# Landing allowances for loads in a kernel's own scheduler: attention and two expert MLPs in fp32 on one Trainium2 core

## The chip, the cores and the metric

The kernel runs on one core of a Trainium2 chip. The metric is the device time of one execution in microseconds (us), as the median of several runs. The engines are named as in the profile: PE is TensorE (matmuls), PEld its weight loads, DVE is VectorE, ACT is ScalarE, POOL is GpSimd, and SP is SyncE, which here only issues transfers (its queue is SPq).

## What is computed

Three steps follow each other; the output of one is the input of the next. The sizes are B=4, H=8, S=576, D=64 for attention, and 2304 tokens, model width 512 and inner width 2048 for both MLPs. All arithmetic is in fp32.

```python
def attention(q, k, v, M_prev, z_prev, beta):
    scores = where(causal, -1e9, q @ k.T / sqrt(D))
    a = exp(scores - scores.max(-1)); a /= a.sum(-1) + 1e-9
    local = a @ v
    q_p = where(q > 0, q, exp(q) - 1) + 1
    mem_out = (q_p @ M_prev) / (q_p @ z_prev + 1e-6)
    g = sigmoid(beta)
    return g * mem_out + (1 - g) * local
def moe(x, w_in, w_out, s, b):
    r = maximum(x @ w_in, 0)
    return (s * r * r + b) @ w_out
def moe2(x, w_in, w_out, a, b):
    h = x @ w_in
    P = a[0] + a[1] * h + a[2] * h**2 + a[3] * h**3
    Q = 1 + abs(b[0]) * abs(h) + abs(b[1]) * h**2
    return (P / (Q + 1e-6)) @ w_out
```

## The kernel before, in words

**Arithmetic.** A fp32 product is made of three matmuls: each operand is split into a high part (a cast, lines 368 and 370) and a low part (the operand minus its high part, line 378, `pair_op`), and high times high, high times low and low times high are summed in PSUM. The weights of both MLPs come as 64-bit raw values. A raw block is one load of 512 KB, 128 x 1024 words (`dAi_..r`, `dAo..r`, `dB_..r`, `d2i_..r`, `d2o..r`). `decode` (from line 405) turns it into 128 x 512 fp32 values with one ACT instruction (line 418, into `..m`), four DVE instructions (lines 419, 421, 423, 425, into `..f`), a cast to the high part and a subtraction for the low part.

**Stages.** From 0 to about 407 us the 32 attention units run (4 batches, low or high queries, 4 pairs of heads): scores `s` (line 657), mask and maximum on DVE (`s,st`, line 664), exponentials `p` on ACT (line 675), transposes `pt`, copies `th`, the sum `av`, and the gated result `xp` on DVE (line 877), which multiplies with `cb`, a row of reciprocals that goes to DRAM (`crow`) and comes back broadcast over partitions. Between them PE runs a filler, block A: the first half of the inner width of MLP 1 for early blocks of 256 tokens (`ha`, line 922; on DVE `ha` at line 939 and `gla` at line 940; `acc`, line 987). Its weights are decoded in the first 110 us (16 raw blocks `dAi`, `dAo`); the other half of these weights is decoded in 16 raw blocks `dB`, one about every 16 us from 124.8 us on, and stored to DRAM. From about 407 us on the rest of block A runs, then block B (the second half of the inner width, 450 to 657 us; `hb`, line 922; `hb` and `glb` on DVE at lines 939 and 940), beside which the raw blocks of MLP 2 (`d2o`, `d2i`) are decoded, then block C (MLP 2, to the end).

**What sets the order.** Nothing in the program issues instructions in the order in which it is written. `Plan.op` (line 109) registers an operation with the engines that may run it (`ways`, each with a cost in us), the buffers it reads and writes, and a place in time (`at`). `Plan.run` then goes through all operations with a clock for every engine. For each engine `choose` takes, among the operations whose inputs have been given out, the one that can start soonest by the reckoned clock (ties by `at`); an operation with several ways is left to another engine if that one would end it sooner. What is chosen is issued at once, so the reckoned times set both the order of each engine's instructions and, for work that ACT, DVE or POOL could do, the engine. The chip then runs each engine's list in order and waits for real data.

A load on SP is reckoned so: SP is taken for 0.48 us; the data's share of the queue is `0.1 + size / 350e3` us; and its readers are ready at `o.end`:

```python
                clock[e] = start + 0.48
                dma = max(dma, start + 1.2) + cost
                o.end = dma + 1.2
```

For a raw block of 512 KB on an idle queue that is 4.0 us after the issue, for a broadcast load of `cb` of 96 KB 2.8 us. There are two buffers for raw blocks, and four PSUM banks (3 to 6) for the upward products `ha`, `hb`, `hc`; a bank of `hb` is given to a later group when DVE's `glb` has read it.

Of the kernel before, what the change touches and what calls it, by code (L numbers as in the profile page):

```python
# [39 lines left out]
}  # L40
PCOPY = False
RAW = 0
ALONE = 8
R0, R1, RN = 0.0, 0.0, 0
ENDS, LEAD, LEADS = 1, 0.7, 384
# [34 lines left out]
class Plan:  # L80
# [25 lines left out]
            t.obj = self.pools[t.place[0]].tile(t.shape, t.dt, tag=t.place[1], name=t.name, bufs=1)  # L106
        return t.obj

    def op(self, ways, fn, r=(), w=(), lag=0.0, port=False):


        o = Op(ways, fn, (self.at, len(self.ops)))
        o.ready = {e: self.since for e in ways}
        o.lag, o.port = lag, port
        keys = [(k, "r") for k in r] + [(k, "w") for k in w]
        keys = [(k if isinstance(k, tuple) else (k, None), x) for k, x in keys]
        deps, seen = set(), set()
        for (name, part), x in keys:
            t = self.bufs[name]
            assert not t.gone, name  # L120
            found = False
            for q, ops in t.did["w" if x == "r" else "r"].items():
                if part is None or q is None or q == part:
                    deps.update(ops)
                    found = True
            assert found or x == "w" or t.const, (name, part)
            if name in seen:
                continue
            seen.add(name)
            if t.before is not None:  # L130
                deps.update(t.before.users)
                t.before.gone = True
            if t.place is not None:
                if t.place[0] == "ps" and not t.users:
                    o.opens.append(t)
                elif t.place[0] == "ps":
                    deps.add(t.users[0])
                if t.place[0] in self.inner:
                    assert self.swap is None
                if t.place[0] in self.outer:  # L140
                    deps.add(self.swap)
        for (name, part), x in keys:
            t = self.bufs[name]
            if o not in t.users[-1:]:
                t.users.append(o)
                o.touch.append(t)
            t.did[x].setdefault(part, []).append(o)
        deps.discard(o)
        o.left = len(deps)
        for d in deps:  # L150
            d.next.append(o)
        self.ops.append(o)
        return o
# [10 lines left out]
    def run(self, engines, nbanks):  # L164
# [40 lines left out]
        for _ in self.ops:  # L205
            cand = [(c[1], c[2].at, e, c[2], c[3]) for e, c in ((e, choose(e)) for e in engines) if c is not None]
            start, _, e, o, b = min(cand, key=lambda c: c[:2])
            for x in o.ways:
                wait[x].remove(o)
            cost = o.ways[e]  # L210
            if e == "PE":
                busy = [x for x in busy if x[1] > start - 4.0]
                if sum(y - max(x, start - 4.0) for x, y in busy) < 2.6:
                    cost *= 2
                busy.append((start, start + cost))
            elif e != "SP":
                cost *= INFL
            if e == "SP":
                clock[e] = start + 0.48
                dma = max(dma, start + 1.2) + cost  # L220
                o.end = dma + 1.2
            else:
                clock[e] = start + cost
                o.end = clock[e] + o.lag
                if e == "POOL" or e == "DVE" and o.port:
                    port = clock[e]
            for t, i in zip(o.opens, b):
                bank_of[i] = t
                t.obj = self.pools["ps"].tile(t.shape, t.dt, tag=f"bank{i}", name=t.name)
            o.start, o.eng = start, e  # L230
            if o is self.swap:
                wait_for[0] = WAIT
            o.fn(engines[e])
            for t in o.touch:
                t.left -= 1
                t.free = max(t.free, o.end)
                if not t.left and t.place is not None and t.place[0] == "ps":
                    i = bank_of.index(t)
                    bank_of[i], bank_free[i] = None, t.free + BGAP
            for n in o.next:  # L240
                for x in n.ways:
                    n.ready[x] = max(n.ready[x], o.end + GAPS[e][x] + (SLACK if x == "PE" != e else 0.0))
                n.left -= 1
                if not n.left:
                    enlist(n)
# [3 lines left out]
def tile_kernel(ctx, tc, qk, vm, z, beta, w1i, w1o, s1, b1, w2i, w2o, a2, b2, out):  # L249
# [104 lines left out]
            t["POOL"] = 0.15 + c * 0.0021 * pool  # L354
        return t

    def load(dst, src, size, r=(), w=(), act=False):

        if act:
            op({"ACT": 0.55}, lambda e: e.dma_start(dst(), src()), r, w, lag=1.7 + size / 360e3)  # L360
        else:
            op({"SP": 0.1 + size / 350e3}, lambda e: e.dma_start(dst(), src()), r, w)  # L362

    def copy(dst, src, c, r, w, act=0.0, dve=1.0, pool=None):

# [41 lines left out]
    def decode(src, nm, hi, lo, key, total=False):  # L407

        ring(f"{nm}r", "raw", [P, 512, 2], I32)
        ring(f"{nm}m", "dm", [P, 512], F32)  # L410
        ring(f"{nm}f", "df", [P, 512], I32)
        R, M, F = f"{nm}r", f"{nm}m", f"{nm}f"
        load(lambda: g(R).rearrange("p f w -> p (f w)"), lambda: src.bitcast(I32), 512 * 1024, (), (R,))

        def top():
            return g(R)[:, :, 1]

        op(ways(512, 0.0), lambda e: e.activation(g(M), f32(top()), AF.Square), (R,), (M,))
        op(ways(512, None, 0.5), lambda e: e.tensor_scalar(
            g(F), top(), 3, 0x3FFFFFF8, ALU.logical_shift_left, ALU.bitwise_and), (R,), (F,), port=True)  # L420
        op(ways(512, None, 1.0), lambda e: e.scalar_tensor_tensor(
            g(F), g(R)[:, :, 0], 29, g(F), ALU.logical_shift_right, ALU.bitwise_or), (R, F), (F,), port=True)
        op(ways(512, None, 1.0), lambda e: e.scalar_tensor_tensor(
            g(F), top(), -0x40000000, g(F), ALU.bitwise_and, ALU.bitwise_or), (R, F), (F,), port=True)
        op(ways(512, None, 1.0), lambda e: e.scalar_tensor_tensor(
            f32(g(F)), g(M), TINY, f32(g(F)), ALU.is_ge, ALU.mult), (M, F), (F,), port=True)
        kh, kl = key
        copy(hi, lambda: f32(g(F)), 512, (F,), (kh,), dve=0.5, pool=0.41)
        pair_op(lo, lambda: f32(g(F)), lambda: f32(hi()), ALU.subtract, 512, (F, kh), (kl,))
        if total:  # L430
            pair_op(lambda: wsum, lambda: wsum, lambda: f32(g(F)), ALU.add, 512, (F, "wsum"), ("wsum",))
# [285 lines left out]
    def phi_b(p):  # L717
# [67 lines left out]
            load(lambda: crow[:, P:P + 64].unsqueeze(0), lambda: g(C1)[2:3].rearrange("o (j q) -> o j q", j=2), 1e4, (C1,), ((CR, 1),))  # L785
        for j in range(2):
            load(lambda j=j: g(CB)[64 * j:64 * j + 64], lambda j=j: crow[j:j + 1, 0:r.nq].to_broadcast([64, r.nq]),
                 64 * 4 * r.nq, (CR,), ((CB, j),))

    def transposes(n):  # L790

# [566 lines left out]
```

## Time and profile before

| | us |
|---|---|
| median of 3 runs | 1059.18 (1057.67 to 1060.86) |
| the profiled execution, its own time | 1057.09 |
| its span in the trace | 1055.1 |
| PE busy | 1016.8 (96% of the span) |
| DVE busy | 840.5 (80%) |
| ACT busy | 691.9 (66%) |
| POOL busy | 416.9 (40%) |
| share of PE on the chain of work that ended last | 69% |
| shares of DVE, DMA and ACT on that chain | 16%, 8%, 3% |

The span is the time from the first to the last instruction of one execution. PE is busy in nearly all of it. The chain of work that ended last is followed back from the last instruction, at each step to what released it; a DMA on it is a transfer for whose landing an engine waited while nothing else held up the end. A wait in a row of the profile is put down to the operation that ended it.

### The profile page before, as it was taken

How to read it: one execution, taken by the hardware profiler on the slowest of the kernel's cores; microseconds unless marked ns; L12 is line 12 of the kernel's file. 1: busy time of each engine (PE TensorE's matmuls, PEld its weight loads, DVE VectorE, ACT ScalarE, POOL GpSimd, SP SyncE). 2: the span in 40 equal slices, each digit the busy share in tenths (PEclk: the TensorE clock that was granted, in tenths of full speed). 3: DMA queues.
4: the chain of work that ended last, by engine and by line, in shares of the span. 5: the costliest groups of instructions: out<-in, count | busy, mean ns of one | idle time of the engine just before them, and what ended most of it. 6: DMA issues, size and time to landing. Idle time of an engine off the chain costs nothing.

```text
span 1055.1 us, 17519 instructions
## 1 busy us (share of the span) xinstructions
PE 1016.8 (96%) x5980; PEld 868.6 (82%) x5980; DVE 840.5 (80%) x1495; ACT 691.9 (66%) x1462; POOL 416.9 (40%) x473
## 2 busy tenths in 40 slices
PE   6879899989999999999999999999999999999998
PEld 4458688878977889987778999888888888898997
DVE  6989877887878875479999543888888888887896
ACT  6977665675557664355554444877866877777896
POOL 2412311122003131012021002877767876876785
PEclk8998999999999999999999999999999999999999
DMA  7766555556646656987765332900200200010000
GB/s 208 220 192 190 162 184 187 171 187 183 208 143 186 202 170 212 341 257 218 239 219 170 103 101 71 318 1 5 73 1 0 70 1 1 23 41 1 30 1 30
DMA packets 88632, 140.41 MB, mean 133 GB/s; under 512 B 12408, under 2 KB 50400, under 8 KB 88544
## 3 DMA queue, kind: packets, MB, share of 16 engines
q1 hardware_dynamic: 83856, 130.52, 39.3%
q0 software_dynamic: 4224, 8.39, 2.6%
q8 instruction: 47, 0.77, 0.3%
q10 hardware_dynamic: 464, 0.40, 0.2%
q14 instruction: 41, 0.34, 0.1%
HBM read 103.56 MB, written 35.71 MB: 132 GB/s over the span
## 4 chain that ended last, share of the span: by engine, by line
PE 69%; DVE 16%; DMA 8%; issue 3%; ACT 3%; SPq 1%; POOL 1%; DVEq 0%; ACTq 0%; POOLq 0%
PE hc L922 19%; PE ac L1113 19%; PE acc L987 7%; PE ha L922 7%; PE ab L1026 5%; PE hb L922 4%; PE av L866 2%; PE pt L525 2%; PE s L657 2%; DMA dAi_1r<-in_w1i 1%; SPq L362 1%; DVE s L664 1%; PE av L874 1%; PE su L691 1%; ACT p L675 1%
## 5 line engine op out<-in xcount | busy, mean ns | idle before, releaser
L1092 DVE RECIPROCAL qe<-qe 128x512 f32<-128x512 f32 (+2 forms) x82 | 242.6, 2959 | 49.5 <-POOL qe L378 49.2
L922 PE MATMUL hc<-xc_h,w2il 128*128 128x512 f32 (+1 forms) x320 | 117.8, 368 | 0.0
L922 PE MATMUL hc<-xc_h,w2ih 128*128 128x512 f32 (+1 forms) x320 | 117.8, 368 | 0.0
L922 PE MATMUL hc<-xc_l,w2ih 128*128 128x512 f32 (+1 forms) x320 | 117.7, 368 | 0.0
L378 POOL TENSOR_TENSOR qe<-qe,qb 128x512 f32<-128x512 f32 (+2 forms) x82 | 94.9, 1157 | 55.3 <-ACT qb L1077 54.5
L1113 PE MATMUL ac<-w2oh,ghc 128*128 128x512 f32 x288 | 112.6, 391 | 0.0
L1113 PE MATMUL ac<-w2ol,ghc 128*128 128x512 f32 x288 | 112.5, 391 | 0.0
L1113 PE MATMUL ac<-w2oh,glc 128*128 128x512 f32 x288 | 112.3, 390 | 0.0
L378 POOL TENSOR_TENSOR glc<-po,ghc 128x512 fp32r<-128x512 f32 (+2 forms) x82 | 94.9, 1157 | 22.9 <-ACT ghc L368 22.8
L378 POOL TENSOR_TENSOR pm<-pm,s 128x512 f32<-128x512 f32 (+2 forms) x82 | 95.2, 1161 | 17.5 <-ACT pm L1077 16.5
L987 PE MATMUL acc<-gha,w1olA 128*128 128x256 f32 x288 | 85.3, 296 | 0.0
L1083 ACT ACTIVATE s<-hc 128x512 f32<-128x512 f32 (+2 forms) x82 | 44.7, 545 | 61.1 <-PE hc L922 58.4
L987 PE MATMUL acc<-gla,w1ohA 128*128 128x256 f32 x288 | 82.6, 287 | 0.6 <-DVE gla L940 0.6
L987 PE MATMUL acc<-gha,w1ohA 128*128 128x256 f32 x288 | 82.5, 287 | 0.0
L675 ACT ACTIVATE p<-s,st 128x128 f32<-128x128 f32 (+3 forms) x128 | 66.6, 529 | 18.2 <-DVE st L664 18.0
L1077 ACT ACTIVATE pm<-hc,prm 128x512 f32<-128x512 f32 (+2 forms) x82 | 59.6, 727 | 22.6 <-DVE hc L1094 21.9
L525 PE MATMUL pt<-ident,p 128*128 128x128 f32 x320 | 59.4, 282 | 12.4 <-ACT th L368 6.2
L922 PEld LDWEIGHTS hc<-xc_h,w2il 128*128 128x128 f32 x320 | 60.1, 188 | 9.0 <-DVE po L1096 0.4
L922 PEld LDWEIGHTS hc<-xc_l,w2ih 128*128 128x128 f32 x320 | 60.1, 188 | 8.6
L922 PEld LDWEIGHTS hc<-xc_h,w2ih 128*128 128x128 f32 x320 | 60.0, 188 | 7.5
L1077 ACT ACTIVATE qb<-s,cq,b1abs 128x512 f32<-128x512 f32 (+2 forms) x82 | 62.7, 765 | 2.1 <-POOL qe L378 2.1
L664 DVE CUSTOM_DVE_ANT_0 s<-s,mask 128x128 f32<-128x128 f32 (+3 forms) x128 | 60.2, 510 | 4.7 <-PE s L657 3.7
(498 smaller groups left out, 2962.8 us busy)
## 6 DMA issues: line engine op xcount, KB each, us to landing
vm<-in_vm SPq DMA_DIRECT2D x16, 384.0 KB, 4.0
k<-in_qk SPq DMA_DIRECT2D x32, 144.0 KB, 3.8
x2p<-ev SPq DMA_DIRECT2D x18, 256.0 KB, 4.4
out_y<-ob SPq DMA_DIRECT2D x18, 256.0 KB, 2.0
qm<-in_vm SPq DMA_DIRECT2D x16, 256.0 KB, 3.1
w1d<-sh SPq DMA_DIRECT2D x16, 256.0 KB, 2.3
w1d<-sl SPq DMA_DIRECT2D x16, 256.0 KB, 2.3
w2d<-sh SPq DMA_DIRECT2D x16, 256.0 KB, 2.9
```

The lines of the kernel that those rows point to most:

```text
L378: op(ways(c, None, dve, pool), lambda e: e.tensor_tensor(dst(), x(), y(), alu), r, w, port=True)
L525: nc.tensor.transpose(dst[:, o:o + P], src, ident)
L657: nc.tensor.matmul(g(b)[:, o2:o2 + kb - ka], g(Q)[m, q], g(K)[m, ka:kb], start=True, stop=True)
L664: e.tensor_tensor_reduce(sp, sp, mask[:, m0:m0 + kb - ka], -scale, 3.0e38 if x == 0 else st[:, t:t + 1], ALU.add, ALU.min, st[:, t + x:t + ...
L675: e.activation(g(f"p{n}_{i}")[:, o:o + kb - ka], g(b)[:, o2:o2 + kb - ka], AF.Exp, scale=-1.0, bias=g(f"st{n}")[:, z_:z_ + 1], accum_out=g ...
L922: nc.tensor.matmul(hs(), m, y, start=c == 0 and k == 0, stop=c == KC - 1 and k == 2)
L987: nc.tensor.matmul(a, outp(y, f)[:, cs], g(z_)[:, us], start=f == 0 and k == 0 and c % 2 == 0, stop=f == HF - 1 and k == 2, skip_group_che ...
L1026: nc.tensor.matmul(g(ACC)[:, 0:w], outp(y, f)[:, cs], g(z_), start=f == 0 and k == 0, stop=f == HF - 1 and k == 2)
L1077: return lambda e: e.activation(g(dst)[:, ks], g(src)[:, ks], AF.Identity, scale=m, bias=b)
L1083: op(ways(c, -0.04), lambda e, ks=ks: e.activation(g(S2)[:, ks], g(HS)[:, ks], AF.Square), (HS,), part(S2))
L1092: op({"DVE": 0.07 + c * 0.00625}, lambda e, ks=ks: e.reciprocal(g(QE)[:, ks], g(QE)[:, ks]), part(QE), part(QE))
L1113: nc.tensor.matmul(g(ACC), g(x_)[:, ks], g(f"w2o{y}{i}")[:, o], start=f == 0 and q == 0, stop=f == NF - 1 and q == 2)
```

## The change

Three constants are added: an operation on SP is reckoned to be ready 0.6 us later (`LANDS`, the default of `load`, so for stores and most loads), a raw weight block 1.6 us later (`LANDS_RAW`), and a load of `cb` 0.8 us later (`LANDS_CB`). Loads that ACT issues keep their reckoning. SP's own clock and the queue's `dma` are unchanged. For a raw block on an idle queue the reckoned landing goes from 4.0 to 5.6 us after the issue.

```diff
+LANDS, LANDS_RAW, LANDS_CB = 0.6, 1.6, 0.8
...
-    def op(self, ways, fn, r=(), w=(), lag=0.0, port=False):
+    def op(self, ways, fn, r=(), w=(), lag=0.0, port=False, late=0.0):
...
-        o.lag, o.port = lag, port
+        o.lag, o.port, o.late = lag, port, late
...
                 dma = max(dma, start + 1.2) + cost
-                o.end = dma + 1.2
+                o.end = dma + 1.2 + o.late
...
-    def load(dst, src, size, r=(), w=(), act=False):
+    def load(dst, src, size, r=(), w=(), act=False, late=LANDS):
...
         else:
-            op({"SP": 0.1 + size / 350e3}, lambda e: e.dma_start(dst(), src()), r, w)
+            op({"SP": 0.1 + size / 350e3}, lambda e: e.dma_start(dst(), src()), r, w, late=late)
...
-        load(lambda: g(R).rearrange("p f w -> p (f w)"), lambda: src.bitcast(I32), 512 * 1024, (), (R,))
+        load(lambda: g(R).rearrange("p f w -> p (f w)"), lambda: src.bitcast(I32), 512 * 1024, (), (R,), late=LANDS_RAW)
...
-                 64 * 4 * r.nq, (CR,), ((CB, j),))
+                 64 * 4 * r.nq, (CR,), ((CB, j),), late=LANDS_CB)
```

No arithmetic is added or removed, and PE keeps its 5355 rows of code. What changes is the order on every engine, and the engine of 184 operations. The new line numbers are higher by one. Up to the tenth `xp` DVE has 342 rows before and 346 now, and among them 10 subtractions into `w1ilA` and `w1olA` (line 378) before and 15 now; the five came from POOL.

**The first raw block, on ACT.** `dAi_0m` is the first instruction that reads raw block `dAi_0r`; `p` are exponentials, `ph` the exponential of q, `rb` a copy of reciprocals, `th` the copies of transposed `p` for which PE waits. Before:

```order
L675 ACTIVATE p_1_248,rs_200<-s_1_0_209,st_197 128x384
L418 ACTIVATE dAi_0m<-dAi_0r 128x512
L675 ACTIVATE p_0_266,rs_267<-s_0_0_223,st_244 128x128
L587 ACTIVATE ph_273<-qm_202 128x384
L368 COPY rb_284<-rec_95 128x2x3x64
L368 COPY th_0_290<-pt_0_275 128x384
L368 COPY th_1_294<-pt_1_280 128x384
```

Now:

```order
L676 ACTIVATE p_1_246,rs_202<-s_1_0_211,st_199 128x384
L676 ACTIVATE p_0_257,rs_258<-s_0_0_225,st_248 128x128
L588 ACTIVATE ph_272<-qm_195 128x384
L419 ACTIVATE dAi_0m<-dAi_0r 128x512
L369 COPY th_0_291<-pt_0_274 128x384
L369 COPY th_1_296<-pt_1_283 128x384
```

One `p` and the `ph` stand ahead of the raw block now, and the copy `rb` has gone to DVE.

**A raw block in the attention stage, on DVE.** `dB_1_2r` is a block of the second half (`dB_2r` in the trace); `ha` and `gla` belong to block A, `xp` to attention, `s,st` are masks and maxima, `fl` a low part. Before:

```order
L877 TENSOR_TENSOR xp_3401<-av_3369,cb_3345 128x384
L378 TENSOR_TENSOR ml_3412<-qm_3069,mh_3403 128x128
L939 SCALAR_TENSOR_TENSOR ha_1_3359<-ha_1_3359,ra_1_3438 128x512
L419 TENSOR_SCALAR dB_1_2f<-dB_1_2r 128x512
L940 TENSOR_TENSOR gla_1_3464<-ha_1_3359,gha_1_3452 128x512
L421 SCALAR_TENSOR_TENSOR dB_1_2f<-dB_1_2r,dB_1_2f 128x512
L664 ISA s_0_0_3454,st_3486<-s_0_0_3454,mask 128x128
```

Now:

```order
L941 TENSOR_TENSOR gla_1_3467<-ha_1_3392,gha_1_3452 128x512
L776 TENSOR_TENSOR fl_3478<-pf_3444,fs_3469 128x384
L665 ISA s_0_0_3455,st_3482<-s_0_0_3455,mask 128x128
L665 ISA st_3482 128x1
L665 ISA s_0_0_3454,st_3465<-s_0_0_3454,mask 128x256
L665 ISA st_3465 128x1
L665 ISA s_0_0_3455,st_3482<-s_0_0_3455,mask 128x256
L665 ISA st_3482 128x1
L665 ISA s_1_0_3471,st_3465<-s_1_0_3471,mask 128x384
L665 ISA st_3465 128x1
L420 TENSOR_SCALAR dB_1_2f<-dB_1_2r 128x512
```

The first instruction that needs the block has gone behind `gla_1`, an `fl` and four masks.

**The first chunk of block B, on DVE.** `d2o..` and `d2i..` are raw blocks of MLP 2. Between `glb_3` and `glb_4` there were 17 rows of decoding, and then `hb_4`; the last rows before:

```order
L421 SCALAR_TENSOR_TENSOR d2o9f<-d2o9r,d2o9f 128x512
L423 SCALAR_TENSOR_TENSOR d2o9f<-d2o9r,d2o9f 128x512
L425 SCALAR_TENSOR_TENSOR d2o9f<-d2o9m,d2o9f 128x512
L939 SCALAR_TENSOR_TENSOR hb_4_6815<-hb_4_6815,rb_4_6847 128x512
L940 TENSOR_TENSOR glb_4_6950<-hb_4_6815,ghb_4_6855 128x512
```

Now `hb_4` stands ahead of 18 rows of decoding (the 17 and the cast `sh_6889`), and `glb_4` behind them; the first and the last rows:

```order
L940 SCALAR_TENSOR_TENSOR hb_4_6811<-hb_4_6811,rb_4_6834 128x512
L379 TENSOR_TENSOR w2il_6855<-d2i_0f,w2ih_6851 128x512
L379 TENSOR_TENSOR sl_6860<-d2o7f,sh_6836 128x512
L420 TENSOR_SCALAR d2o8f<-d2o8r 128x512
...
L424 SCALAR_TENSOR_TENSOR d2o9f<-d2o9r,d2o9f 128x512
L426 SCALAR_TENSOR_TENSOR d2o9f<-d2o9m,d2o9f 128x512
L941 TENSOR_TENSOR glb_4_6947<-hb_4_6811,ghb_4_6853 128x512
```

On PE 48 matmuls stand between the last of `hb_4` and the first of the next chunk, which needs the bank that `glb_4` frees, in both versions.

## Rows read from the trace of the kernel before

**Rows 1.** Windows: stretch, length, busy PE, PEld, DVE, ACT, POOL, PEclk, DMA share, GB/s.

```profile
0.00:140.00 140.00, 116.00 (x763) 87.34 (x765) 120.94 (x365) 102.72 (x291) 38.53 (x78) 0.93 0.66 194
140.00:407.00 267.00, 259.31 (x2046) 223.04 (x2042) 203.12 (x595) 168.39 (x446) 50.15 (x108) 0.99 0.57 177
407.00:660.00 253.00, 250.41 (x1373) 224.78 (x1372) 180.08 (x287) 120.15 (x206) 34.07 (x28) 1.00 0.61 199
```

**Rows 2.** Timeline of PE: start, length, what; idle before it, and what ended that.

```profile
16.84 1.54 PE L525 MATMUL pt<-ident,p 128*128 128x128 f32 x6 [4.35 <-ACT th L368]
132.35 2.37 PE L657 MATMUL s<-k,q 64*128 64x128 f32 x10 [2.46 <-DVE xp L877]
234.14 0.92 PE L657 MATMUL s<-k,q 64*128 64x384 f32 x4 [1.63 <-DVE gla L940]
303.88 0.38 PE L987 MATMUL acc<-gla,w1ohA 128*128 128x256 f32 x1 [0.63 <-DVE gla L940]
310.27 0.39 PE L922 MATMUL ha<-xa5h,w1ilA 128*128 128x256 f32 x1 [1.30 <-ACT p L675]
487.58 0.50 PE L922 MATMUL hb<-xb_h,w1ilB 128*128 128x512 f32 x1 [0.83 <-DVE glb L940]
510.98 0.50 PE L922 MATMUL hb<-xb_h,w1ilB 128*128 128x512 f32 x1 [0.93 <-DVE glb L940]
```

**Rows 3.** Windows behind four of these waits, columns as in rows 1.

```profile
133.60:136.80 3.20, 3.20 (x13) 2.15 (x11) 3.20 (x11) 0.93 (x2) 0.40 (x1) 0.52 0.44 152
235.60:239.00 3.40, 3.40 (x17) 3.03 (x18) 3.40 (x11) 3.03 (x10) 0.54 (x2) 0.51 0.38 99
...
487.60:494.00 6.40, 6.40 (x28) 5.30 (x29) 6.12 (x9) 3.78 (x7) 0.90 (x1) 1.00 0.83 264
...
310.30:317.00 6.70, 6.70 (x63) 6.15 (x65) 4.34 (x14) 4.93 (x15) 0.62 (x2) 1.00 0.67 207
```

**Rows 4.** The chain that ended last, around raw blocks: start, length, what.

```profile
7.88 6.68 DMA dAi_0r<-in_w1i
...
124.84 5.81 DMA dB_0r<-in_w1i
...
131.74 0.56 DVE xp L877
...
227.19 5.84 DMA dB_2r<-in_w1o
...
233.40 0.69 DVE gla L940
...
295.63 5.94 DMA dB_2r<-in_w1i
```

**Rows 5.** Timeline of ACT around the first raw block, columns as in rows 2.

```profile
14.57 0.68 ACT L418 ACTIVATE dAi_0m<-dAi_0r 128x512 f32<-128x512 f32 x1 [2.68 <-DMA dAi_0r<-in_w1i]
...
15.90 0.51 ACT L368 COPY rb<-rec 128x384 f32<-128x384 f32 x1
16.30 0.87 ACT L368 COPY th<-pt 128x384 f32<-128x384 f32 x2
```

**Rows 6.** Timeline of DVE and ACT in block B, first chunk, columns as in rows 2.

```profile
474.94 0.68 DVE L940 TENSOR_TENSOR glb<-hb,ghb 128x512 fp32r<-128x512 f32 x1
475.54 0.68 DVE L378 TENSOR_TENSOR sl<-d2o7f,sh 128x512 fp32r<-128x512 f32 x1
...
475.90 0.60 ACT L935 ACTIVATE rb<-hb 128x512 f32<-128x512 f32 x1 [0.23 <-PE hb L922]
...
482.37 0.43 DVE L370 CAST w2ih<-d2i_0f 128x512 fp32r<-128x512 f32 x1
...
486.03 0.69 DVE L939 SCALAR_TENSOR_TENSOR hb<-hb,rb 128x512 f32<-128x512 f32 x1
486.83 0.69 DVE L940 TENSOR_TENSOR glb<-hb,ghb 128x512 fp32r<-128x512 f32 x1
```

**Rows 7.** DMA issues: out<-in, queue, operation, count, KB each, median us to landing.

```profile
cb<-crow SPq DMA_DIRECT2D x24, 96.0 KB, 3.1
...
d2i_2r<-in_w2i SPq DMA_DIRECT2D x4, 512.0 KB, 3.8
d2i_3r<-in_w2i SPq DMA_DIRECT2D x4, 512.0 KB, 4.0
```

## The prediction

> **What bounds the kernel now.** I read four views. The windows by stage come first [rows 1]: they show how much PE idles in each stage, since a change that only moves work can win no more than that. In the first 140 us PE is busy for 116.00 us, so 24.0 us are idle; from 140 to 407 us 7.7 us are idle; from 407 to 660 us 2.6 us. In the first stage DVE is busy for 120.94 of 140 us, more than PE: there, and only there, DVE and PE share the bound. Behind 660 us block C keeps PE busy, its raw blocks have been decoded long before, and I expect nothing from it.
>
> The second view is PE's timeline, for what ended each wait [rows 2]. The largest waits with a name are 4.35 us at 16.84 (ACT's copies `th`), 2.46 us at 132.35 (`xp` on DVE), 1.63 us at 234.14 (`gla` on DVE), 0.63 and 1.30 us at 303.88 and 310.27, and in block B 0.83 and 0.93 us (`glb`).
>
> The third view shows the price that stands behind a wait [rows 3]. After the waits of 2.46 and 1.63 us the granted clock was 0.52 and 0.51 for 3.20 and 3.40 us, which is the 1.2 GHz level; after those of 1.30 us (310.27) and 0.83 us (487.58) it stayed at 1.00, the 2.4 GHz level. PE was busy through both half-clock stretches, so each cost half its length, about 1.6 to 1.7 us, on top of the wait.
>
> The last view is the chain of waits [rows 4]. It shows who was late in the first place: raw blocks. `dB_0r` landed 5.81 us after its issue, `dB_2r` 5.84 and 5.94 us. The scheduler reckoned 4.0. In the list of DVE an instruction that reads the block stood ahead of `xp` (131.74) and of `gla` (233.40), so these waited for a transfer that they don't need, and PE for them. The first block, `dAi_0r`, took 6.68 us.
>
> **The change part by part**, against the profiled execution of 1057.09 us, which lies 2.1 us below the median of 1059.18.
>
> *First raw block.* `dAi_0m` starts at 14.57, when the block lands [rows 5]. It stays ahead of the copies `th`, so the 2.68 us of waiting on ACT stay too: 6.68 us are more than the 5.6 now reckoned. But between it and the first `th` stood a `p`, `ph` and the copy `rb`, until 16.30; these now stand ahead of it or are gone to DVE. With 0.68 us for `dAi_0m`, `th` could start at 15.25 instead of 16.30: **−1.05**. The bounds are −1.05 and 0 (if PE is then late for another reason).
>
> *Raw blocks in the attention stage.* The waits that hang on them are 2.46 + 1.63 + 0.63 + 1.30 = 6.02 us [rows 2], and two half-clock stretches of 3.20 and 3.40 us cost half their length, 3.3 us [rows 3]; together 9.3. The allowance of 1.6 takes the reckoning to 5.6, against 5.81 to 5.94 measured [rows 4], so about 1.6 of 1.85 us of lateness are provided for. The order shows the effect: before `dB_1_2r` is first read, `gla_1`, `fl` and four masks are now run. I take three quarters, **−7.0**, since a wait that goes uncovers the next limit at some of the four places: DVE, with the decode then behind. The bounds are −9.3 and 0.
>
> *Work given to DVE early.* Of the subtractions into block A's weights five more stand on DVE in the stretch to the tenth `xp`. At 0.68 us each [rows 6] that is 3.4 us. DVE is the busier engine there, but PE was idle for 24.0 of 140 us [rows 1] for several reasons; I count a third, **+1.0**. The bounds are 0 and +3.4.
>
> *Block B, first chunk.* Before, 17 decoding instructions ran on DVE from 475.54 to 486.03, 10.5 us, then `hb_4` (0.69) and `glb_4` at 486.83, and PE waited 0.83 us for that [rows 2, 6]. Now `hb_4` is first. It needs `rb`, which ACT ends at 475.90 + 0.60 = 476.50; so DVE, which in the old order would decode at that time, waits until then. Then come `hb_4` (0.6), the 17 instructions (10.5) and a cast (0.43): `glb_4` starts at 488.1 instead of 486.8, **+1.3**. PE's 48 matmuls between are the same, so its wait grows from 0.83 to about 2.1 us. That is over the 1.63 after which the clock fell, so I add a half-clock stretch, **+1.7**. Together +3.0; the bounds are 0 (the transfers and ACT put DVE elsewhere by then) and +4.3 (another 1.3 at the second such place).
>
> *The other two allowances.* `cb` landed 3.1 us after the issue in the median [rows 7], the reckoning goes from 2.8 to 3.6; for most loads and stores 0.6 are added. No wait of the list above has such a transfer as its cause, and the filler of block A covers a reader that is put later; I cost them at nothing. Without that cover, where block A has no weights yet, an `xp` moved behind one more DVE instruction of 0.68 us would cost that.
>
> The sum is −1.05 − 7.0 + 1.0 + 3.0 = −4.05: 1053.0 for the profiled execution, and 2.1 more for the median, **1055.1 us**.
>
> In block B the raw blocks landed in 3.8 to 4.0 us [rows 7]: there the old reckoning of 4.0 was right, and an allowance of 1.6 only makes the scheduler put other things first. The Trainium skill ("DMA: Bandwidth & Descriptors", section "Anatomy of one DMA — SWDGE (gpsimd) path") speaks for that view everywhere: it gives a transfer about 2.0 us plus its bytes over 436 GB/s, by which a block of 512 KB takes an estimated 3.2 us, and no allowance would be needed. The attention stage's 5.81 to 5.94 us in this trace disagree; block B's 3.8 to 4.0 are nearest to it.
>
> **The rivals.**
>
> *All of it comes back and nothing is paid.* −1.05 − 9.3 = −10.35, with the median 1048.8. For it: each of the waits has a transfer in its chain. Against it: the later DVE order in block B and the five subtractions are visible in the lists.
>
> *Nothing is won.* Three of the four attention waits are replaced by others (DVE's decode, now later, holds its buffer, of which there are two, and the next block's load starts late). Then a third of the 9.3 is left, and the sum is −1.05 − 3.1 + 1.0 + 3.0 = −0.15: 1059.0. For it: from 140 to 407 us PE idles only 7.7 us and DVE 63.9, so the stage is near PE's bound, and its order is dense.
>
> *Slower: decode in front of `glb`.* The mechanism is DVE's order in block B. If the `glb` of both places, at 487.58 and 510.98 [rows 2], comes behind a run of decoding as long as the one shown, each costs 3.0; with the five subtractions in full the sum is 6.0 + 3.4 − 1.05 − 3.1 = +5.25, 1064.4. It decides from the point where PE's wait at `glb_4` passes 1.6 us (the clock falls), at both places, and where less than a third of the attention stage's 9.3 comes back. Against it: only the first place has such a run in the lists.
>
> *Raw blocks take no longer than reckoned, but for accidents.* If the lateness of 5.8 us belongs to what else was in flight at those moments, another order meets other blocks late, and the allowances win nothing: only +1.0 + 3.0 are left, 1063.2. Blocks of 3.8 to 4.0 us in block B speak for it; three late ones out of those on the chain speak against it. The rule of the Trainium skill named above, of 2.0 us plus bytes, would have it so.
>
> **How the numbers follow.** A measurement of this kernel can tell about 0.3%, 3.2 us, so "faster" begins below 1056.0 and "slower" above 1062.4. The forecast case has a chance of 0.40; in its own spread (attention's part −5 to −9.3) it runs from 1057.1 to 1052.8, and I put 0.28 of it below 1056.0 and 0.12 within. All won: 0.18, faster. Nothing won: 0.20, within. Decode in front of `glb`: 0.17, and accidents: 0.05, both slower. Sums: faster 0.46, same 0.32, slower 0.22. The range goes from 1048.5, the case in which all is won, to 1064.0, just under the slower case's price; outside lie a part of that case and orders better or worse than any bound here.
>
> **What would show it.** In the changed profile PE's waits for `xp` and `gla` near 132, 234 and 304 us should be gone or below 1 us, with a granted clock of 1.00 behind them; PE's first long wait should shrink from 4.35 to about 3.3 us; PE should be idle some 2.5 us in 140 to 407 us; and a wait of about 2.1 us for `glb` should stand near 485 us with half a clock behind it. I am wrong if waits of over 1.6 us still stand between 140 and 407 us, if the raw blocks there land in under 5 us, or if block C changes its length.

## The result, and the profile after

The changed kernel takes 1049.74 us (median of 6 runs, 1048.34 to 1050.74), the kernel before in the runs beside it 1060.68 us (6 runs, 1057.67 to 1064.9). The ratio is 0.9901, with a 95% interval of 0.9882 to 0.9921. The change is faster by 1.0%, about 10.5 us; 1055.1 had been forecast, with a range from 1048.5 to 1064.0.

The profiled execution of the change took 1050.74 us and is 6.35 us below that of before, 1057.09. This pair shows less than the medians, since the profiled execution of before lies 3.6 us below the median of its six runs and that of the change 1.0 above; a second profile of the kernel before (below) took 1059.27.

The first part of the page of the changed kernel, and the windows by stage, in the columns of [rows 1]:

```profile
PE 1009.1 (96%) x5980; PEld 865.7 (83%) x5980; DVE 847.2 (81%) x1501; ACT 687.0 (66%) x1451; POOL 417.0 (40%) x478
```

```profile
0.00:140.00 140.00, 114.53 (x807) 88.84 (x807) 126.28 (x374) 101.99 (x287) 41.66 (x89) 0.96 0.66 196
140.00:407.00 267.00, 263.20 (x2095) 227.83 (x2094) 209.44 (x600) 172.19 (x452) 51.27 (x105) 1.00 0.62 188
407.00:660.00 253.00, 246.60 (x1306) 220.65 (x1305) 179.48 (x285) 117.47 (x202) 33.33 (x29) 0.99 0.60 196
660.00:1048.70 388.70, 384.80 (x1778) 328.42 (x1776) 332.00 (x245) 295.35 (x513) 290.73 (x256) 1.00 0.10 34
```

From 140 to 407 us PE idles for 3.8 us instead of 7.7. In the first window the granted clock is 0.96 instead of 0.93, and 807 matmuls are done instead of 763. From 407 to 660 us it is the other way: 6.4 us idle instead of 2.6.

PE's timeline names the waits, in the columns of [rows 2]. These are the longest between 5 and 100 us, two of the longest between 107 and 407 us, and the one in block B:

```profile
18.48 1.54 PE L526 MATMUL pt<-ident,p 128*128 128x128 f32 x6 [6.23 <-ACT th L369]
58.29 0.39 PE L923 MATMUL ha<-xa0h,w1ilA 128*128 128x256 f32 x1 [3.06 <-ACT p L676]
78.15 0.30 PE L526 MATMUL pt<-ident,p 128*128 128x128 f32 x1 [2.44 <-DVE gla L941]
214.99 0.39 PE L923 MATMUL ha<-xa3h,w1ilA 128*128 128x256 f32 x1 [0.70 <-ACT p L676]
363.24 0.38 PE L923 MATMUL ha<-xa6h,w1ilA 128*128 128x256 f32 x1 [0.70 <-ACT p L676]
481.85 0.79 PE L923 MATMUL hb<-xb_h,w1ilB 128*128 128x512 f32 x1 [6.24 <-DVE glb L941]
```

All the waits of [rows 2] behind raw blocks are gone; between 107 and 407 us none is over 0.70 us. In their place stands one of 6.24 us in block B.

To see where time went although the order differs, I use the count of matmuls in the trace (5980 in every version) as milestones: the 700th, 2800th and 4200th, at 127.5, 406.4 and 665.6 us before. The stretches between them hold nearly the same matmuls in all versions: in the first two, 3 are others in the change and at most 19 in any version; in the last two none. The stretches are called start, attention, block B and block C (from the 4200th to the last matmul). The windows of the attention stretch of before and of the change, columns as in [rows 1]:

```profile
127.50:406.40 278.90, 268.74 (x2103) 230.36 (x2102) 211.94 (x620) 175.34 (x467) 50.80 (x110) 0.99 0.58 179
```

```profile
126.50:395.10 268.60, 264.80 (x2103) 227.49 (x2102) 214.51 (x627) 175.17 (x467) 51.80 (x110) 1.00 0.61 185
```

Nearly the same 2103 matmuls take 10.3 us less: PE idles 3.8 us instead of 10.2, and is busy 3.9 us less; 3.4 of these are half of the 6.8 us at half clock, which are gone. The other stretches between the two profiles: start −1.0, block B +5.0 (264.2 against 259.2), block C 385.1 in both.

### The profile page after: what moved, and what is told of

Same layout as the page of the kernel before. It is cut to its first block, busy times and chain, and to the rows that moved or that the text cites. A ratio compares the mean times of both kernels' runs of the same rounds, so it can differ in the third digit from the quotient of the medians.

```text
span 1048.8 us, 17526 instructions
## 1 busy us (share of the span) xinstructions
PE 1009.1 (96%) x5980; PEld 865.7 (83%) x5980; DVE 847.2 (81%) x1501; ACT 687.0 (66%) x1451; POOL 417.0 (40%) x478
## 4 chain that ended last, share of the span: by engine, by line
PE 75%; DVE 12%; DMA 6%; ACT 3%; issue 2%; SPq 1%; POOL 0%; ACTq 0%; DVEq 0%
PE hc L923 19%; PE ac L1114 19%; PE ha L923 9%; PE acc L988 7%; PE ab L1027 6%; PE hb L923 5%; PE av L867 3%; PE pt L526 2%; PE s L658 2%; DMA w2d<-sh 2%; DVE s L665 1%; SPq L363 1%; PE av L875 1%; DMA qm<-in_vm 1%; DMA cb<-crow 1%
## 5 line engine op out<-in xcount | busy, mean ns | idle before, releaser
L923 PE MATMUL hb<-xb_h,w1ilB 128*128 128x512 f32 (+1 forms) x160 | 59.3, 370 | 6.2 <-DVE glb L941 6.2
```

The costliest lines, as they stand in the source:

```text
L923: nc.tensor.matmul(hs(), m, y, start=c == 0 and k == 0, stop=c == KC - 1 and k == 2)
```

## The experiments

**One allowance alone.** In the changed kernel, `late` is kept for the blocks `dB` and set to 0 for all else, so no other load has an allowance.

```diff
-LANDS, LANDS_RAW, LANDS_CB = 0.6, 1.6, 0.8
+LANDS, LANDS_RAW, LANDS_CB = 0.0, 1.6, 0.0
...
-        load(lambda: g(R).rearrange("p f w -> p (f w)"), lambda: src.bitcast(I32), 512 * 1024, (), (R,), late=LANDS_RAW)
+        load(lambda: g(R).rearrange("p f w -> p (f w)"), lambda: src.bitcast(I32), 512 * 1024, (), (R,), late=LANDS_RAW if nm.startswith("dB") else 0.0)
```

> The kernel before with one allowance alone: 1.6 us for the 16 raw blocks dB of the attention stage, nothing for any other load. Its order is that of before up to about 112 us, and near the end of block B again. Theory A (the raw blocks that land 5.8 to 5.9 us after the issue are what held PE in the attention stage): the waits at 132, 234, 304 and 310 us go with their two half-clock stretches, 9.3 us in all, and block B stays as before: 8 to 10 us faster than before, about 1050. Theory B (the attention stage got faster because the whole order is another one, whatever the allowance of these blocks): within 3 us of before. Theory C (the landing is an accident of the moment, and blocks are late elsewhere in another order): other waits on raw blocks of over 1.5 us stand between 112 and 407 us, and no more than 4 us are won.

Measured: 1060.95 us, ratio 1.0017 (0.9999 to 1.0035). Nothing is won; attention took 281.0 us. PE's waits there:

```profile
133.68 1.49 PE L658 MATMUL s<-k,q 64*128 64x128 f32 x6 [2.35 <-DVE xp L878]
274.25 0.33 PE L526 MATMUL pt<-ident,p 128*128 128x128 f32 x1 [1.94 <-DVE gla L941]
375.72 0.33 PE L526 MATMUL pt<-ident,p 128*128 128x128 f32 x1 [1.97 <-DVE gla L941]
```

The waits at 234 and 304 to 310 us went as theory A says, but there are new ones, and that at 132 us stayed with another cause. DVE's timeline ahead of the first two:

```profile
133.07 0.56 DVE L878 TENSOR_TENSOR xp<-av,cb 128x384 f32<-128x384 f32 x1 [4.36 <-DMA cb<-crow]
...
268.21 0.43 DVE L371 CAST xa5h<-xa5r 128x512 fp32r<-128x512 f32 x1 [2.62 <-DMA xa5r<-xTd]
```

With the raw block out of the way, `xp` waits 4.36 us for `cb`, and at 268 us DVE waits 2.62 us for the block `xa5r` and is late with the decoding and with `gla`. Ahead of the third, at 375.72, DVE waited for no load in the 5 us before; `gla` stands there behind four rows of decoding, one of which took 1.59 us. Theory A falls, since nothing is won. B's number came true (within 3 us of before), so this run doesn't rule B out, though the waits at 234 and 304 to 310 us did go with the allowance. C falls in its form: two of the new waits are behind other kinds of load, the third behind none.

**No allowance for the second MLP's blocks, none for raw blocks, and decoding later.** The second of these leaves the constants at `0.6, 0.0, 0.8`; the first and the third are

```diff
-        load(lambda: g(R).rearrange("p f w -> p (f w)"), lambda: src.bitcast(I32), 512 * 1024, (), (R,), late=LANDS_RAW)
+        load(lambda: g(R).rearrange("p f w -> p (f w)"), lambda: src.bitcast(I32), 512 * 1024, (), (R,), late=0.0 if nm.startswith("d2") else LANDS_RAW)
```

```diff
-DEC = 20.0
+DEC = 0.0
```

> The changed kernel with no allowance for the raw blocks of the second MLP (d2o, d2i), all else as changed. The order is that of the change up to about 370 us. In its list 26 decoding rows of DVE stand ahead of glb_4 of the first chunk of block B (24 in the change, 17 before). Theory A (the 6.24 us wait at 481.85 us comes from the run of decoding ahead of glb_4, which the order of the whole stage sets): the wait stays, 5 to 7 us, and the time is within 2 us of the change. Theory B (it comes from the allowance of the second MLP's blocks itself): the wait is back at about 0.8 us and the time is 5 to 6 us below the change.

> The changed kernel without the allowance for raw blocks; 0.6 us for other loads and 0.8 us for cb stay. Theory A (the raw blocks' allowance wins the attention stage): waits of over 1 us behind raw blocks are back between 112 and 407 us, and with 26 decoding rows ahead of glb_4 block B loses 5 to 7 us: slower than before by 0 to 7 us. Theory B (the general allowance of 0.6 us or that of cb wins it): attention is as fast as in the change, and the time is within 3 us of the change.

> The changed kernel with the constant DEC at 0 instead of 20, which gives the decoding of the second MLP's blocks a later place among operations that could start at the same time; nothing else. The order is that of the change up to about 370 us. At most 8 decoding rows stand ahead of any glb of the first chunk of block B (24 in the change). Theory A (the run of decoding ahead of glb_4 costs 5.4 us of wait and about 2.5 us of half clock there): the wait at 482 us is under 1 us, the clock stays at 1.00, and the time is 5 to 8 us below the change, about 1043. Theory B (PE would wait there anyway, for the bank of an earlier product or for ACT, or the decoding that is put off is missed later, at the start of block C): within 2 us of the change.

Measured: 1050.56 us without the second MLP's allowance (ratio 0.9922, 0.9903 to 0.9942), as the change. 1064.96 without raw allowances (1.0050, 1.0033 to 1.0068). 1045.9 with later decoding (0.9870, 0.9848 to 0.9891). The wait for `glb` in the first and the second of them, of which the lists have 26 decoding rows ahead of `glb_4`:

```profile
481.71 0.79 PE L923 MATMUL hb<-xb_h,w1ilB 128*128 128x512 f32 x1 [5.96 <-DVE glb L941]
```

```profile
490.60 0.79 PE L923 MATMUL hb<-xb_h,w1ilB 128*128 128x512 f32 x1 [4.92 <-DVE glb L941]
```

With at most 8 rows ahead no such wait stands near 482 us, and block B takes 258.9 us instead of 264.2. The whole is 3.8 us below the change, though, where 5 to 8 had been expected: the attention stretch took 271.4 us there, 2.8 more than in the change, and in block B part is lost later, where the put-off decoding is in the way:

```profile
531.91 0.50 PE L1027 MATMUL ab<-glb,w1ohB 128*128 128x512 f32 x1 [1.75 <-DVE glb L941]
577.13 0.50 PE L1027 MATMUL ab<-glb,w1ohB 128*128 128x512 f32 x1 [1.06 <-DVE glb L941]
```

So the run of decoding is the cause of the wait in block B, and the allowance of those very blocks is not. The version with DEC at 0 has the lowest time of all. Its interval and that of the change (0.9882 to 0.9921) still touch; that of the version beside it which has the same wait as the change (0.9903 to 0.9942) it doesn't reach.

The run without raw allowances came in as slower by the stated amount, but only in part for the stated reason. One wait of PE behind a raw block is back: 2.30 us at 148.62 for a `th`, ahead of which ACT waited 2.15 us for `dB_1r`. Yet its attention stretch took 273.7 us, about 5 less than before. The loss that shows is in block B, 4.7 us; its start of 131.5 us lies within those of before's order (127.5 to 132.1, below).

**Allowances added from 112 us on.** The blocks `dB` have 1.6; `cb`, general loads, or both have theirs, but only where they are registered at place 95 or later and before the end of attention. So the first 112 us are those of before.

```diff
+        if late < 1.0 and not 95.0 <= plan.at < END:
+            late = 0.0
```

> The kernel before with 1.6 us for the raw blocks dB and 0.8 us for the loads of cb that are registered from the tenth unit or so on (place 95 or later), no other allowance. The order is that of before up to about 112 us; block B has the 17 decoding rows of before ahead of glb_4. Theory D (a load that is reckoned too early holds an engine wherever it stands next, so each allowance only moves the wait to the next load that has none): with cb allowed for, the wait of 2.35 us at 133.68 that the run with dB alone had goes, with its half clock (4 us), while waits behind xa loads, which have no allowance here, remain or appear: last av group at 400 to 405 us (407.30 with dB alone, 403.79 before), time 1053 to 1057. Theory E (the attention stage's gain is a matter of which order happens to come out): no relation to the causes named; the last group at 405 us or later.

> The same with 0.6 us for general loads and stores (place 95 to the end of attention) in place of the 0.8 us for cb. Theory D: the wait for cb near 133 us stays (2 us and its half clock), those behind the xa loads near 274 and 375 us go: last av group at 400 to 405 us, and block B costs more where 24 decoding rows stand ahead of glb_3: time 1055 to 1062. Theory E: no relation, the last group at 405 us or later.

> The same with all three allowances, from place 95 to the end of attention; block B has none. The order is that of before up to about 112 us. Theory D: no wait of over 1.2 us is left between 112 and 407 us; the last av group starts at 394 to 397 us, 7 to 10 us ahead of before. In block B 22 decoding rows stand ahead of glb_4, so 4 to 7 us are lost there as in the change: time 1052 to 1056. Theory E: the last av group within 4 us of before.

> The kernel before once more, for a second profile of it. Theory A (the waits behind raw blocks belong to this order): waits of over 1 us stand again at 132 and 234 us and near 304 to 310 us, each within 0.7 us of the first profile's 2.46, 1.63 and 1.93. Theory C (they are accidents of one execution): at least two of the three are under 0.5 us, and others stand elsewhere.

Measured: 1056.44 us with cb (0.9974, 0.9959 to 0.9988), 1066.49 with general loads (1.0081, 1.0051 to 1.0111), 1056.86 with both (0.9979, 0.9964 to 0.9995). The last `av` group starts at 403.49, 405.90 and 404.68 us. With cb the wait near 134 us shrinks from 2.35 to 0.44 us and without cb it is there (2.43), and with the general allowance the one at 274 us is gone, as theory D says; the one near 375 us, though, is there with it (1.81), and that run misses its numbers (400 to 405 and 1055 to 1062). And with all three it forecast 394 to 397 us, and missed by 8: waits of 1.26 us (at 135.71, for the load `xa2r` itself), 1.00 (at 220.55) and 2.13 us (at 375.47) are left there. The last of these stands behind no load: DVE is busy all along with decoding and masks ahead of a `gla`. So theory D holds for single waits, but not for the sum; and the last groups of the second and the third run, at 405 us or later and within 4 us of before, are what theory E had said. With all three allowances from 112 us on, attention won 1.9 us by the table below, and why so much less than with allowances from the start is open.

Block B missed its number in the third run too. It took 259.8 us, as before, where 4 to 7 us were to be lost behind 22 decoding rows; the wait for `glb_4` is a third of the change's:

```profile
489.67 0.59 PE L925 MATMUL hb<-xb_h,w1ilB 128*128 128x512 f32 x1 [1.87 <-DVE glb L943]
```

So the count of rows alone doesn't give the wait. In the second run, with 24 rows ahead of `glb_3`, it was 4.01 us, and block B took 266.4.

The kernel before, profiled again, shows the same waits in the same places, though the first is 0.79 us shorter, just outside the 0.7 allowed, and only that one has half a clock behind it. Theory C is out:

```profile
134.12 2.30 PE L657 MATMUL s<-k,q 64*128 64x128 f32 x10 [1.67 <-DVE xp L877]
235.36 0.93 PE L657 MATMUL s<-k,q 64*128 64x384 f32 x4 [1.48 <-DVE gla L940]
305.05 0.39 PE L987 MATMUL acc<-gla,w1ohA 128*128 128x256 f32 x1 [0.34 <-DVE gla L940]
311.45 0.39 PE L922 MATMUL ha<-xa5h,w1ilA 128*128 128x256 f32 x1 [1.30 <-ACT p L675]
```

In block B of this execution the wait for `glb_4` was 2.01 us instead of 0.83, and the clock behind it stayed at 1.00:

```profile
490.34 0.50 PE L922 MATMUL hb<-xb_h,w1ilB 128*128 128x512 f32 x1 [2.01 <-DVE glb L940]
```

```profile
490.40:494.00 3.60, 3.60 (x16) 2.97 (x17) 3.43 (x6) 1.88 (x4) 0.00 (x0) 1.00 0.68 214
```

**The size, and raw blocks alone.** Constants `0.0, 1.6, 0.0`, then `0.9, 2.4, 1.2`, then `0.4, 1.1, 0.5`.

> The changed kernel with the 1.6 us for all raw blocks alone (the first stage's and the second MLP's too), 0 for general loads and for cb. The stretch from the 700th to the 2800th matmul of the trace (about 127 to 400 us) took 278.9 us before and 268.6 in the change. Theory A (the raw blocks' allowance wins this stretch): 268 to 271 us. Theory D (waits go only where all late loads are allowed for): 274 to 280 us, with waits of over 1 us behind cb or xa loads. In block B at most 5 decoding rows stand ahead of glb_4 but 20 ahead of glb_3; a wait of 1 to 5 us there.

> The changed kernel with all three allowances half as large again (0.9, 2.4 and 1.2 us). Theory F (what matters is that the reckoned landings are no earlier than the real ones): the stretch from the 700th to the 2800th matmul takes 267 to 271 us, and since at most 9 decoding rows stand ahead of the first chunk's glb, block B's long wait is gone: 1042 to 1049 in all. Theory E (the order of the change is a lucky draw, any other set of numbers gives another one): 273 us or more in this stretch.

> The changed kernel with all three allowances about a third smaller (0.4, 1.1 and 0.5 us): 5.1 us reckoned for a raw block where 5.8 to 5.9 were measured. Theory F (the reckoned landings must be no earlier than the real ones): some waits behind raw blocks are left, 271 to 276 us from the 700th to the 2800th matmul. Theory G (any part of the allowance has its part of the effect): two thirds of the gain, 271 to 273 us. Theory E (lucky draw): anything from 268 to 282 us with no relation. In block B 19 decoding rows stand ahead of glb_3: a wait of 1 to 5 us.

Measured: 1052.87 us (0.9940, 0.9919 to 0.9960), 1057.07 (0.9974, 0.9955 to 0.9993), 1053.4 (0.9946, 0.9928 to 0.9964). The attention stretch, with PE's idle time and the time at half clock in it, of every version, from the trace:

| allowances (other, raw, cb) | attention, us | idle | half clock |
|---|---|---|---|
| none: before, and again | 278.9, 277.9 | 10.2, 10.1 | 6.8, 3.4 |
| none, decoding later | 278.3 | 10.9 | 3.4 |
| dB alone | 281.0 | 10.5 | 6.8 |
| dB and general, from 112 us | 278.4 | 8.6 | 6.8 |
| all raw blocks, nothing else | 277.1 | 6.8 | 6.8 |
| dB, general and cb, from 112 us | 276.5 | 10.2 | 0.0 |
| dB and cb, from 112 us | 275.5 | 9.2 | 0.0 |
| general and cb, no raw | 273.7 | 7.0 | 0.0 |
| all three, half more | 270.9 | 4.4 | 0.0 |
| all three, a third less | 270.0 | 5.4 | 0.0 |
| all three, decoding later | 271.4 | 5.8 | 0.0 |
| all three (the change; no d2 allowance) | 268.6, 269.3 | 3.8, 4.6 | 0.0 |

With all three from the start the stretch took 268.6 to 271.4 us in five profiles, with three sizes and three orders that part within the first 25 us; in all others, 273.7 to 281.0, and among these is the one with all three from 112 us on (276.5). Theory E, a lucky draw, forecast 273 us or more for half more: it falls for this set of numbers. So does G: two thirds of the size gave nearly the whole gain. Raw blocks alone came out at 277.1, as theory D had it; but the only wait of over 1 us there, 1.87 at 219.71, stands behind a raw block, `dB_1r`, for which ACT waited until 218.53, 6.41 us after its issue, and not behind a `cb` or `xa` load. Theory F's "no earlier than the real ones" is stricter than what is needed, since 5.1 us reckoned for a raw block sufficed.

In the whole time the last two of the three runs are worse than the change: the start took 130.4 and 130.5 us against 126.5, and block B of the larger one 264.4, where its longest run of decoding, 20 rows, stands one chunk later:

```profile
510.33 0.80 PE L923 MATMUL hb<-xb_h,w1ilB 128*128 128x512 f32 x1 [5.27 <-DVE glb L941]
```

The expectation counted the first chunk's runs only, so its 1042 to 1049 us were wrong. For `glb_3` of the first chunk, waits of 1 to 5 us were expected in the other two: with 19 rows ahead it was 2.22 us, with 20 rows (raw blocks alone) there was none over 0.5.

**Later decoding without allowances**, `DEC = 0.0` in the kernel before.

> The kernel before with DEC at 0 and no allowance: the order is that of before up to about 370 us; at most 7 decoding rows stand ahead of the first chunk's glb (17 before). Theory A (DEC only takes away waits for glb in block B, of which before has 2.6 us of idle PE in all and no half clock): the stretch from the 2800th to the 4200th matmul takes 257 to 259 us against 259.2, the time is 0 to 2 us below before, about 1058, so the run with both owes its time to the allowances in attention. Theory B (DEC by itself, not the allowances, makes the run with both the fastest): 1050 or less.

Measured: 1059.62 us, ratio 0.9994 (0.9977 to 1.0011); block B 258.7 us. Theory A holds, within the interval (0 to 2 us below before had been expected; it came out 0.4 above the runs beside it): what the fastest version wins over before comes from the allowances, and DEC only keeps block B from giving it back.

## Why the prediction was right, and where its sums were off

The direction held, the time lies in the range, and the two main terms, attention and block B, came out with the signs forecast. But the gain is 2.6 times the 4.05 us of the sum: attention gave 1.6 us more than forecast and block B took 2.0 more, and 4 us came from the start, where the forecast had none. That the total still fell in the range is partly luck. "Same order" means the profiles of kernels whose order is that of before up to about 112 us (seven of them), and up to about 370 us that of the change (three: the change, no d2 allowance, later decoding).

- **Raw blocks in attention, −7.0.** Measured −8.6: 278.4 as a mean of before, its second profile and later decoding without allowances, against 269.8 for the change, the run without d2 allowance and later decoding. That is near the upper bound, −9.3: the named waits and both half-clock stretches went, and no wait of over 1.06 us took their place. The step that was wrong is the cause: 1.6 us for raw blocks were to do this, and **"the other two allowances"** to do nothing. The runs show that dB's allowance alone wins nothing, that of all raw blocks 1.3 us (277.1), and 0.6 and 0.8 us without it 4.7 (273.7). These don't add up to 8.6, so what each is worth depends on the others. What had no wait of its own in the list of before, `cb` and `xa`, was next in line. The chain of before had shown it: a `cb` at 250.62 and an `xa4r` at 257.41 are on it, for which DVE waited 0.72 and 2.02 us.

```profile
176.85 4.97 DMA dB_3r<-in_w1i
...
250.62 3.58 DMA cb<-crow
254.87 2.48 DMA xTd<-xp
257.41 3.42 DMA xa4r<-xTd
...
332.12 3.80 DMA dB_0r<-in_w1o
...
554.54 5.99 DMA d2i_2r<-in_w2i
574.74 3.83 DMA d2i_3r<-in_w2i
```

- **Late in attention, on time in block B.** This contrast was drawn too sharply. The same chain has a raw block of 3.80 us in attention and one of 5.99 in block B, and the 3.8 and 4.0 of [rows 7] are each known from one of four loads. Where an engine of the kernel before waited for a raw block, that had landed 3.80 to 5.94 us after its issue in attention (eight blocks, median 5.15) and 3.35 to 5.99 in block B (16, median 3.9). In the change it was 4.81 to 6.26 in attention (five blocks); two of them are under the 5 us named as a sign of being wrong. The shortest and the longest of these, as issue on SP and first reader on ACT:

```profile
123.58 0.58 SPq L363 DMA_DIRECT2D dB_0r<-in_w1i  x1
128.42 0.70 ACT L419 ACTIVATE dB_0m<-dB_0r 128x512 f32<-128x512 f32 x1 [1.21 <-DMA dB_0r<-in_w1i]
...
238.13 0.35 SPq L363 DMA_DIRECT2D dB_3r<-in_w1o  x1
244.41 0.69 ACT L419 ACTIVATE dB_3m<-dB_3r 128x512 f32<-128x512 f32 x1 [1.06 <-DMA dB_3r<-in_w1o]
```

  The median of 5.15 us in attention fits that 5.1 reckoned was enough above.
- **The first raw block, −1.05.** Wrong in sign. Moving `ph` ahead of the block put another late load in front. ACT's timeline of the change:

```profile
16.98 0.52 ACT L588 ACTIVATE ph<-qm 128x384 f32<-128x384 f32 x1 [4.50 <-DMA qm<-in_vm]
17.41 0.65 ACT L419 ACTIVATE dAi_0m<-dAi_0r 128x512 f32<-128x512 f32 x1
17.96 0.85 ACT L369 COPY th<-pt 128x384 f32<-128x384 f32 x2
```

  `qm` had been issued at 8.65, between the first two raw blocks (8.18 and 9.13), and landed 8.30 us later by the chain of waits; `th` starts at 17.96 instead of 16.30, and PE waits 6.23 instead of 4.35 us. The size varies: the two other profiles of this order have 4.87 and 4.80 us, seven of before's 3.96 to 5.09, so it is 0.8 us in the mean.
- **Work given to DVE early, +1.0.** Not to be seen apart. The whole start, forecast at −0.05, took 125.0 to 126.5 us in three profiles of the change's order against 127.5 to 132.1 in seven of before's: 4.2 us less in the mean. PE's idle time in it is no smaller (22.6 to 25.5 us against 21.5 to 26.0); the time at half clock is, 13.7 us in the mean against 20.0, and half of the difference is 3.1 us. The other orders with allowances took 126.7 to 131.5 us, in no relation to their size, so this part of the gain can't be put down to the allowances as such; why this order has fewer half-clock stretches there is open.
- **Block B, first chunk, +3.0.** Measured +5.0 between the two profiles. The place and the mechanism are as forecast; the wait was 6.24 instead of 2.1 us. From the start of `rb` to `glb_4` it took 16.35 us instead of 10.93 [rows 6], 5.4 more, as much as the wait grew; 12.1 had been reckoned. What was missed is that between `glb_3` and `glb_4` there are 24 rows of decoding now and not 18: six more stand ahead of `hb_4`. DVE, ACT and POOL there:

```profile
466.35 0.43 DVE L371 CAST sh<-d2o7f 128x512 fp32r<-128x512 f32 x1 [0.82 <-DMA w2d<-sh]
...
467.30 0.69 DVE L940 SCALAR_TENSOR_TENSOR hb<-hb,rb 128x512 f32<-128x512 f32 x1
...
475.56 1.38 DVE L371 CAST w2ih<-d2i_0f 128x512 fp32r<-128x512 f32 x1
476.97 1.63 DVE L379 TENSOR_TENSOR w2il<-d2i_0f,w2ih 128x512 fp32r<-128x512 f32 x1
...
481.11 0.68 DVE L941 TENSOR_TENSOR glb<-hb,ghb 128x512 fp32r<-128x512 f32 x1
```

```profile
464.76 0.60 ACT L936 ACTIVATE rb<-hb 128x512 f32<-128x512 f32 x1 [3.52 <-PE hb L923]
```

```profile
474.84 3.22 POOL L379 TENSOR_TENSOR xb_l<-xb_r,xb_h 128x512 fp32r<-128x512 f32 x2 [16.87 <-DMA d2o9r<-in_w2o]
```

  `hb_4` starts 2.54 us behind the start of `rb` and not 0.6, since those six rows are ahead of it and one, a cast, waited 0.82 us for a store: 1.9 us. The run of 18 rows takes 13.05 us and not 10.9, since a cast and a subtraction ran beside a subtraction on POOL and took 1.38 and 1.63 us instead of 0.43 and 0.68: 1.9 us. The two make nearly all of the difference between 2.1 and 6.24. Behind it the clock was 0.51, and cost 2.5 us, half of 5.05 busy:

```profile
480.10:486.90 6.80, 5.05 (x12) 3.99 (x13) 6.52 (x12) 3.61 (x6) 0.00 (x0) 0.51 0.70 201
```

  The later waits of before, 0.93 us at 510.98 [rows 2] the largest of them, are gone; so block B as a whole has 6.4 us idle against 2.6, and lost 5.0. That a wait of over 1.6 us brings half a clock, as the term of 1.7 us and the slower rival took it, is not what the runs show: behind waits of 2.01 (490.34, before again), 2.13 (375.47, dB, general and cb) and 2.30 us (148.62, no raw allowance) the clock stayed at 1.00, and before itself has 0.53 behind one of 1.14 us (last section).
- **Of the rivals**, the first, in which all of attention comes back and nothing is paid, gave nearly the time measured, by other sums: nearly all came back, more was paid than forecast, and the start won 4. The second falls, since 8.6 and not 3.1 us came back. The slower one has its mechanism confirmed at one place; it did not decide, as no second place followed. The fourth, by which lateness is an accident of the moment, falls in its result, since the allowances won; but which blocks are late does differ between the orders. The rule of the Trainium skill ("DMA: Bandwidth & Descriptors", section "Anatomy of one DMA — SWDGE (gpsimd) path"), by which no allowance would be needed, is given there for transfers that GpSimd issues, and these loads go out from SP. Its estimate of 3.2 us lies below every landing of a raw block read from these two profiles, 3.35 us at the least.

The stretches add up to −4.2 − 8.6 + 5.0 = −7.8 us; the ratio of the runs says −10.5, with an interval from −12.5 to −8.4, so 0.6 to 4.7 us are not accounted for by these profiles.

## What to carry to other kernels

In a kernel whose order comes from reckoned times, a load that is reckoned too early holds up every instruction behind its first reader. Look for all kinds of load that land later than reckoned, not only for those behind which the trace shows a wait: correct one, and the next in line takes its place, as it did here with dB alone. In the orders tried here attention won 7 us and more only where all of them were corrected from the start of the kernel on; the reason for that is open. And read the new order for long runs of side work ahead of an instruction that frees a bank, in all chunks; a small change in priorities can take them away, and gave 1045.9 us here.

## What was not expected of the hardware

The same order of the first 112 us took 127.5 to 132.1 us to the 700th matmul in seven profiles, with 13.7 to 27.3 us at half clock: the wait of 1.14 us at 61.61 of before has half a clock behind it (0.53), the same one of the run with dB and cb, nearly as long, has not (1.00). Timeline of PE and window behind it, of before and then of that run:

```profile
61.61 0.47 PE L525 MATMUL pf<-ident,ph 128*128 128x128 f32 x1 [1.14 <-ACT th L368]
```

```profile
61.80:65.20 3.40, 3.40 (x24) 2.57 (x23) 1.58 (x6) 1.82 (x6) 0.95 (x2) 0.53 0.98 284
```

```profile
63.27 0.33 PE L528 MATMUL pf<-ident,ph 128*128 128x128 f32 x1 [1.07 <-ACT th L371]
```

```profile
63.40:66.80 3.40, 2.05 (x25) 1.63 (x25) 1.75 (x6) 1.93 (x6) 1.01 (x2) 1.00 0.96 290
```

Some DVE instructions of 128x512 took two to three times as long beside a 128x512 subtraction on POOL: the cast and the subtraction above 1.38 for 0.43 and 1.63 for 0.68 us. Others kept their time: `glb` of before at 486.83 [rows 6] took 0.69 us, although POOL ran such subtractions from 485.45 to 488.51. And loads of `cb` of 96 KB, with a median of 3.1 us [rows 7], once took 5.65 us, on the chain of the run with dB's allowance alone.
